# Two partial sums kept apart in a planned attention and MLP kernel: plain stores and a VectorE add for accumulating DMAs, and other landing times in its scheduler

## The chip, the cores and the metric

The kernel runs on one core of a Trainium2 chip. The metric is the device time of one execution in microseconds (us). The engines are named as the profile names them: PE is TensorE (matmuls; PEld are its weight loads), DVE is VectorE, ACT is ScalarE, POOL is GpSimd, and SP is SyncE, which here only issues DMAs.

## The reference

A linear attention block is followed by an MLP with softplus. In sizes: 8 batches, 8 heads, 576 tokens, 64 per head, so 4608 tokens of 512 features; `w_in` is 512 x 2048 and `w_out` 2048 x 512.

```
kv  = einsum('bhsd,bhse->bhde', k, v)
o   = einsum('bhsd,bhde->bhse', q, kv)
x   = o / sqrt(mean(o*o, -1) + 1e-6) * g_norm      # heads joined: 4608 x 512
h   = x @ w_in
g   = max(h, 0) + log1p(exp(-abs(h)))              # softplus
out = g @ w_out                                     # 4608 x 512, float32
```

## The kernel before

**Numbers in three parts.** The large matrices are kept as three parts of type float32r (a high part, the rest, and a correction), made by one ACT operation and two DVE operations, and every large product sums matmuls of such parts in PSUM. The weights come as 64-bit floats. A fetch (L398, 512 KB for a piece of 128 x 512) is followed by a chain on ACT and DVE (L409 to L439) that makes a float32 of them, and by the split.

**Three phases.** The 2048 columns between the two products are cut into 16 chunks of 128.

- The head loads q, k, v and the first weights. For each batch PE sums kv (L671), for each tile of 128 tokens it makes the rows of o (L695), then ACT, DVE and POOL normalise them and PE turns them (L713, L751). This work goes on beside the first phase.
- The first phase (ph 0, function `step`) goes over 12 blocks of 384 tokens, and in each over chunks 0 to 3 (blocks 0 to 3) or 0 to 5 (the others). A step is 12 matmuls for h (L838), softplus and split on ACT and DVE (L849, L853, L860, L862), and 9 matmuls into the sums of three tiles (L845).
- The second and third phases (ph 1 and 2, function `wide_step`; `LAST` is 2) go over 9 blocks of 512 tokens, and in each over pairs of the remaining chunks: 27 steps in the second phase, 21 in the third. A step makes h for two chunks by seven block products (L1025, 42 matmuls) with ACT copies in between (L1049, L1066, L1070) and a DVE add (L1074), then softplus (L1052), the split (L1082, L1085, L1088), and 24 matmuls into the sums of four tiles (L1095). The operands of the seven products are made by `units_of` (loads at L935, split at L985 to L991).

**Partial sums.** A tile's sum (128 x 512 in float32, one PSUM bank) is complete after three phases. `leave` takes a bank to SBUF with ACT (L886). In the first phase SP stores it to a DRAM tile (L906). In the second phase POOL adds it to that DRAM tile with an accumulating DMA (L902). In the third phase `enter` first loads the tile from DRAM (L880, on SP) and ACT copies it into the bank (L881); the matmuls add to it, and `leave` scales and stores the output (L896 or L906). SBUF tiles of 128 x 512 for all of this, for weights and for x come from one ring `m` of 8 slots.

**The planner.** No order is written by hand. Every operation is entered with `add(engine, ns, run, after, pos, take, give, size, ...)`: its engine, its assumed cost, what it depends on, a position `pos`, and the buffer slots that it takes and gives back. `Plan.order` simulates the engines with these costs and, on each engine, starts among the tasks that can start about first the one of lowest `pos`. The instructions are issued in that order, so each engine's queue is fixed when the program is built. For a DMA the planner keeps one clock for all transfers:

```
if t.size:
    dma_free = max(dma_free, at + t.ns) + t.size
    t.end = dma_free + 2000
```

`size` is the time that the transfer is taken to need; `t.end` is when its data count as landed. An SP load into the ring `m` may only start while more than `KEEP` = 4 slots are free. The positions come from lists of tuned numbers, `P0` (weights and head), `P1`, `P2` (later weights) and `P3` (the wide steps). Where the planner finds PE idle for 400 ns in the head, it puts a warm-up matmul (L1176).

Of the kernel before, what the change touches and what calls it, by code (L numbers as in the profile page):

```python
# [8 lines left out]
F32 = mybir.dt.float32  # L9
# [4 lines left out]
ALU = mybir.AluOpType  # L14
# [4 lines left out]
P = 128  # L19
# [36 lines left out]
class Plan:  # L56
# [5 lines left out]
    READY = {"PE": 2500, "ACT": 2500, "DVE": 4000, "POOL": 2500, "SP": 700}  # L62
    SWITCH = {("all", "rows"): 90, ("all", "kv"): 90, ("rows", "all"): 250, ("kv", "all"): 250, ("rows", "kv"): 140, ("kv", "rows"): 140}
    TOGETHER, PATIENCE = 1, 0.0
    KEEP = 4
    BEGIN = 4000
    SOON = 150
# [7 lines left out]
    def slot(self, ring):  # L75
        return Slot(ring)

    def add(self, engine, ns, run, after=(), pos=0.0, take=(), give=(), size=0, behind=None, follows=None, kind="all"):
        t = Task(engine, ns, run, [a for a in after if a is not None], pos, list(take), list(give), size)
        for s in t.give:  # L80
            s.readers += 1
        self.tasks.append(t)
        t.follows = follows
        t.behind = behind
        t.kind = kind
        return t

    def order(self):
# [30 lines left out]
        dma_free = 1500  # L119
# [3 lines left out]
        while left:  # L123
            best = None
            for engine, tasks in ready.items():
                options = []
                for t in tasks:
                    at = max(engine_free[engine], t.ready)
                    if t.size:
                        at = max(at, dma_free - 2500)  # L130
                    for i, s in enumerate(t.take):
                        others = sum(u.ring == s.ring for u in t.take[:i])
                        if engine == "SP" and s.ring in ("m", "n"):
                            others += self.KEEP
                        if len(free[s.ring]) <= others:
                            break
                        at = max(at, sorted(free[s.ring])[sum(u.ring == s.ring for u in t.take[:i])][0])
                    else:
                        options.append((at, t))
                if not options:  # L140
                    continue
                first = min(at for at, _ in options)
                options = [(at, t) for at, t in options if at <= first + self.SOON]
                small = [o for o in options if engine == "PE" and o[1].kind != "all"]
                if small:
                    rest = [o for o in options if o[1].kind == "all"]
                    if kind != "all":
                        options = [o for o in small if o[1].kind == kind] or small
                    elif rest and len(small) < self.TOGETHER and (
                            min(o[1].pos for o in small) + self.PATIENCE > min(o[1].pos for o in rest)):  # L150
                        options = rest
                at, t = min(options, key=lambda o: (o[1].pos, o[0]))
                if engine == "PE" and self.spare and self.spare[-1].start is None:
                    ring, run, ns, _ = self.spare
                    begin = max(engine_free["PE"], self.BEGIN, min(free[ring])[0] if free[ring] else at)
                    if begin + ns <= at:
                        s = Slot(ring)
                        at, t = begin, Task("PE", ns, lambda s=s: run(s), [], None, [s], [s], 0)
                        t.kind = "all"
                        s.readers = 1  # L160
                if best is None or at < best[0]:
                    best = (at, t)
            if best is None:
                raise RuntimeError("the plan is stuck at " + str([(e, t.pos, [s.ring for s in t.take if not free[s.ring]]) for e, ts in ready.items() for t in ts][:20]))
            at, t = best
            if t in ready[t.engine]:
                ready[t.engine].remove(t)
                left -= 1
            for s in t.take:
                place = min(free[s.ring])  # L170
                free[s.ring].remove(place)
                s.place = place[1]
                if t.pos is not None:
                    coming[s.ring] = coming.get(s.ring, 0) - 1
            if t.engine == "PE":
                t.ns += self.SWITCH.get((kind, t.kind), 0)
                kind = t.kind
            t.start = at
            engine_free[t.engine] = at + t.ns
            t.end = at + t.ns + self.HANDOVER[t.engine]  # L180
            if t.size:
                dma_free = max(dma_free, at + t.ns) + t.size
                t.end = dma_free + 2000
            for s in t.give:
                s.readers -= 1
                last_read[id(s)] = max(last_read.get(id(s), 0), t.end)
                if not s.readers:
                    free[s.ring].append((last_read[id(s)], s.place))
                    retire(s.ring)
            for u in users.get(id(t), ()):  # L190
                waiting[id(u)] -= 1
                if not waiting[id(u)]:
                    u.ready = max([a.end for a in u.after] + ([u.follows.start] if u.follows else []), default=0)
                    ready.setdefault(u.engine, []).append(u)
            done.append(t)
# [4 lines left out]
def kernel(  # L200
# [24 lines left out]
    nc = tc.nc  # L225
    B, H, S, D = q.shape
    d_model, d_ff = moe_w_in.shape
# [17 lines left out]
    STEPS = [(ph, n, p) for ph in (1, 2) for n in range(n_wide) for p in PAIRS[ph - 1][n]]  # L245
    LAST = 2

    P0 = [-49.84, -17.88, -35.99, -11.25, -19.79, -5.76, -6.59, 2.32, -72.59, -44.84, -44.11, -27.86, -36.42, -23.37, -11.42, -1.64, 8.39, -28.07, 13.62, 9.21, 8.15, 12.69, -9.98, 5.3, 1.39, 25.83, -11.96, 7.88, 13.2, 7.36]
    CONVERT, FETCH, EARLY, LATER = P0[:8], P0[8:16], P0[16:27], P0[27:]
    P1 = [50.98, 57.72, 60.23, 40.06, 110.11, 134.41, 41.79, 46.64, 73.31, 91.73, 127.74, 138.75]  # L250
    P2 = [23.23, 37.56, 36.87, 47.12, 56.32, 61.0, 53.55, 123.6, 69.05, 107.19, 42.49, 16.95, 48.29, 68.01, 98.48, 79.47, 86.8, 80.78, 146.51, 128.13, -4.65]
    P3 = [2.14, 1.08, 5.88, -0.92, 1.63, 2.67, 2.6, 1.59, 2.29, 2.01, 3.35, 0.34, -0.08, -0.89, 3.05, -0.96]
    SPLIT = {p: (P1[i], P1[6 + i]) for i, p in enumerate((2, 3, 4, 5, 6, 7))}
    TAKEN = {c: (P2[c - 6], P2[4 + c]) for c in range(6, 16)}
    LEAD, APART, AHEAD, MM2, LATE, SPLIT_G = P3[0], P3[1], P3[2], P3[3:11], P3[11:14], P3[14]
# [10 lines left out]
    dram = ctx.enter_context(tc.tile_pool(name="dram", bufs=1, space=DRAM))  # L266
# [39 lines left out]
    slot, add = plan.slot, plan.add  # L306
# [513 lines left out]
    part = {}  # L820
# [54 lines left out]

    def enter(t, bank, pos):

        pt = slot("m")
        src, st = part[t]
        ld = add("SP", 350, lambda: nc.sync.dma_start(out=new(pt, [P, d_model]), in_=src), [st], pos - 2.5, [pt], [], 900, behind=pos - 3.5)  # L880
        return add("ACT", 600, lambda: nc.scalar.copy(new(bank, [P, d_model]), pt.tile), [ld], pos, [bank], [pt])  # L881

    def leave(ph, t, bank, done, pos):

        ot = slot("m")
        a = add("ACT", 690 if ph == LAST else 600, lambda: nc.scalar.activation(  # L886
            new(ot, [P, d_model]), bank.tile, func=AF.Copy, scale=scale if ph == LAST else 1.0),
            [done] + (scale_done if ph == LAST else []), pos, [ot], [bank])
        if ph == LAST and BY_PE <= t < n_tiles - TB:
            n, i = divmod(t, TB)  # L890

            def store():
                for m in range(P // BL):
                    a, u = divmod(P // BL * i + m, TB)
                    row = n * NT + u * P + a * BL
                    nc.sync.dma_start(out=out[row:row + BL], in_=ot.tile[m * BL:(m + 1) * BL])  # L896

            add("SP", 1600, store, [a], pos, [], [ot], 750)
            return
        if ph == 1:  # L900
            dst, st = part[t]
            part[t] = dst, add("POOL", 1000, lambda: nc.gpsimd.dma_start(out=dst, in_=ot.tile, accum_op=ALU.add),  # L902
                               [a, st], pos, [], [ot], 1900)
            return
        dst = out[t * P:(t + 1) * P] if ph == LAST else dram.tile([P, d_model], F32, name=f"part_{t}")
        part[t] = dst, add("SP", 350, lambda: nc.sync.dma_start(out=dst, in_=ot.tile), [a], pos, [], [ot], 720)  # L906

    unit_slots, unit_done = {}, {}

# [234 lines left out]
    for c in range(KF):  # L1144
        for j in (2 * c, 2 * c + 1):
            if c < OWN:
                pos = CONVERT[j] if c < 4 else LATER[c - 4] + LATER[2] * (j % 2)
# [64 lines left out]
```

## Time and profile before

| | us |
|---|---|
| median of 3 runs | 882.69 (879.84 to 883.61) |
| profiled execution | 884.47 |
| its span, first to last instruction | 882.7 |
| first L838 (head ends) | 44.3 |
| first L1025 (second phase begins) | 364 |
| first bank filled again by L881 (third phase begins) | 658.5 |
| last matmul ends | 878.8 |

The phases overlap by a step or so. Rows of the profile give busy time in us, mean ns of one instruction, and idle time of the engine just before, with what ended it. Where the profile gives a stretch of time, it lists for each engine the busy us in it, the granted clock of PE as a share of full speed, and the DMA engines' busy share.

### The profile page before, as it was taken

What the parts mean: (1) busy time and instruction counts of PE and PEld (TensorE: products, weight loads), DVE (VectorE), ACT (ScalarE), POOL (GpSimd) and SP (SyncE); (2) the same over time, 40 slices, a digit from 0 to 9 for tenths busy, and PEclk for the clock granted to TensorE, in tenths of its full rate; (3) what the DMA queues carried; (4) which work ended last, traced back from release to release, by engine and by line L of the source; (5) the groups of instructions that cost most, each with busy time, mean ns of one, the idle gap of its engine ahead of it and who ended that gap; (6) DMA issues with size and microseconds to landing.
All of it is one profiled execution on the core that took longest, in us unless ns stands there. A gap on an engine that the chain in (4) does not pass through costs nothing.

```text
span 882.7 us, 16941 instructions
## 1 busy us (share of the span) xinstructions
PE 861.5 (98%) x6457; PEld 758.8 (86%) x6457; DVE 682.9 (77%) x956; ACT 538.7 (61%) x1015; POOL 111.8 (13%) x115
## 2 busy tenths in 40 slices
PE   7899999999999999999999998999999999999998
PEld 5587888889888899888898887989898888988886
DVE  6798888887878888898889896777887756676652
ACT  5776555444544568666658654556778755666764
POOL 0434223132113100001101100101100000000000
PEclk9999999999999999999999999999999999999999
DMA  9999999859893775537765856846745633566643
GB/s 252 264 199 297 241 221 262 143 179 197 261 165 98 191 215 177 157 105 185 196 186 136 202 153 175 197 128 155 173 132 132 194 96 119 183 193 183 193 120 86
DMA packets 234448, 157.62 MB, mean 179 GB/s; under 512 B 105728, under 2 KB 197888, under 8 KB 234368
## 3 DMA queue, kind: packets, MB, share of 16 engines
q1 hardware_dynamic: 229024, 147.11, 61.3%
q0 software_dynamic: 5184, 9.44, 7.0%
q8 instruction: 50, 0.82, 0.4%
q14 instruction: 30, 0.25, 0.1%
q10 hardware_dynamic: 160, 0.00, 0.0%
HBM read 103.55 MB, written 52.95 MB: 177 GB/s over the span
## 4 chain that ended last, share of the span: by engine, by line
PE 88%; DMA 5%; DVE 3%; ACT 2%; issue 1%; POOL 1%; SPq 0%; DVEq 0%; ACTq 0%
PE banks L1095 30%; PE banks L1025 27%; PE banks L838 14%; PE banks L845 13%; PE banks L695 2%; DMA g<-in_moe_w_out_dram 2%; PE banks L671 2%; DMA raw<-in_moe_w_in_dram 1%; DMA raw<-in_moe_w_out_dram 1%; DMA early<-in_q_dram 1%; PE banks L713 1%; DMA loads<-in_v_dram 1%; POOL r L703 0%; PE banks L751 0%; DVE half L707 0%
## 5 line engine op out<-in xcount | busy, mean ns | idle before, releaser
L1095 PE MATMUL banks<-pieces,gv 128*128 128x512 f32 x624 | 196.0, 395 | 0.0
L1025 PEld LDWEIGHTS banks<-units,pieces 128*128 128x128 f32 x1140 | 151.5, 191 | 16.5 <-ACT banks L1070 6.2
L1025 PE MATMUL banks<-units,pieces 128*128 128x256 f32 x1140 | 158.3, 284 | 4.4 <-ACT banks L1070 3.1
L845 PE MATMUL banks<-pieces,gv 128*128 128x512 f32 x576 | 147.3, 397 | 0.2 <-DVE gv L853 0.2
L838 PE MATMUL banks<-units,pieces 128*128 128x384 f32 x768 | 145.9, 338 | 0.0
L838 PEld LDWEIGHTS banks<-units,pieces 128*128 128x128 f32 x768 | 134.7, 188 | 5.0
L845 PEld LDWEIGHTS banks<-pieces,gv 128*128 128x128 f32 x576 | 105.8, 188 | 21.0 <-DVE gv L853 0.5
L1095 PE MATMUL banks<-pieces,g_False 128*128 128x512 f32 x312 | 122.7, 393 | 0.1
L1095 PEld LDWEIGHTS banks<-pieces,gv 128*128 128x128 f32 x624 | 105.6, 190 | 11.8
L1085 DVE TENSOR_TENSOR gv<-g_True,gv 128x1024 fp32r<-128x1024 f32 x48 | 58.8, 1225 | 67.0 <-ACT gv L1082 66.8
L860 ACT ACTIVATE half<-banks 128x384 f32<-128x384 f32 x64 | 31.3, 489 | 76.4 <-PE banks L838 75.9
L902 POOL DMA_DIRECT2D part<-m x36 | 31.4, 901 | 324.7 <-ACT m L886 289.9
L1095 PEld LDWEIGHTS banks<-pieces,g_False 128*128 128x128 f32 x312 | 58.7, 188 | 13.9 <-ACT banks L1066 0.5
L703 POOL TENSOR_TENSOR r<-r,half 128x8 f32<-128x8 f32 x36 | 64.9, 1804 | 3.0
L1052 ACT ACTIVATE g_True<-banks 128x256 f32<-128x256 f32 x96 | 36.7, 383 | 44.5 <-PE banks L1025 43.0
L1074 DVE TENSOR_TENSOR g_True<-banks,g_True 128x512 f32<-128x512 f32 x48 | 33.1, 689 | 37.9 <-PE banks L1025 24.0
L1088 DVE SCALAR_TENSOR_TENSOR g_False<-gv 128x1024 fp32r<-128x1024 f32 x48 | 58.8, 1225 | 1.6
L985 ACT ACTIVATE units<-loads 128x1024 fp32r<-128x1024 f32 x42 | 44.5, 1059 | 21.3 <-PE banks L1025 17.5
L988 DVE TENSOR_TENSOR units<-loads,units 128x1024 fp32r<-128x1024 f32 x42 | 51.3, 1221 | 5.5 <-ACT units L985 5.3
L991 DVE SCALAR_TENSOR_TENSOR units<-units 128x1024 fp32r<-128x1024 f32 x42 | 51.3, 1222 | 1.4
L1082 ACT ACTIVATE gv<-g_True 128x1024 fp32r<-128x1024 f32 x48 | 50.9, 1060 | 1.0
L886 ACT ACTIVATE m<-banks 128x512 f32<-128x512 f32 x72 | 41.7, 596 | 13.7 <-PE banks L1095 7.5
(117 smaller groups left out, 1370.3 us busy)
## 6 DMA issues: line engine op xcount, KB each, us to landing
loads<-x SPq DMA_DIRECT2D x180, 128.0 KB, 2.7
loads<-form SPq DMA_DIRECT2D x45, 256.0 KB, 3.1
part<-m SPq DMA_DIRECT2D x36, 256.0 KB, 3.3
form<-loads SPq DMA_DIRECT2D x36, 256.0 KB, 3.0
part<-m POOLq DMA_DIRECT2D x36, 256.0 KB, 5.2
m<-part SPq DMA_DIRECT2D x36, 256.0 KB, 3.0
raw<-in_moe_w_in_dram SPq DMA_DIRECT2D x16, 512.0 KB, 5.5
loads<-in_k_dram SPq DMA_DIRECT2D x32, 256.0 KB, 4.8
```

Of the source, the lines that this page charges most:

```text
L703: nc.gpsimd.tensor_tensor(out=r.tile, in0=r.tile, in1=half, op=ALU.pow)
L838: nc.tensor.matmul(hp, lhsT=w_in.tile[:, i, kd * P:(kd + 1) * P], rhs=xv.tile[:, i, kd], start=(m == 0), stop=(m == 3 * KD - 1))
L845: nc.tensor.matmul(mine[i].tile, lhsT=gv.tile[:, m, i * P:(i + 1) * P], rhs=w_out.tile[:, m], start=(c == cs[0] and m == 0), stop=(c == cs ...
L886: a = add("ACT", 690 if ph == LAST else 600, lambda: nc.scalar.activation(new(ot, [P, d_model]), bank.tile, func=AF.Copy, scale=scale if p ...
L985: nc.scalar.activation(part_of(0, F32R), xl.tile if m > 1 else xl.tile[:, 0], func=AF.Copy, scale=DOWN)
L988: nc.vector.tensor_tensor(out=part_of(1, F32R), in0=xl.tile if m > 1 else xl.tile[:, 0], in1=part_of(0), op=ALU.subtract)
L991: nc.vector.scalar_tensor_tensor(out=part_of(2, F32R), in0=part_of(1), scalar=-RADIX, in1=part_of(0), op0=ALU.mult, op1=ALU.add)
L1025: nc.tensor.matmul(place(q), lhsT=w[:, m, at:at + P], rhs=dst.tile[:, m, v, kd] if u < 6 else dst.tile[:, m, kd], start=(u == 0 and not m ...
L1082: nc.scalar.activation(gvt(0, F32R), gt(), func=AF.Copy, scale=DOWN)
L1085: nc.vector.tensor_tensor(out=gvt(1, F32R), in0=gt(), in1=gvt(0), op=ALU.subtract)
L1088: nc.vector.scalar_tensor_tensor(out=gt(F32R), in0=gvt(1), scalar=-RADIX, in1=gvt(0), op0=ALU.mult, op1=ALU.add)
L1095: nc.tensor.matmul(mine[i].tile, lhsT=(gvt(m, F32R) if m < 2 else gt(F32R))[:, c, i * P:(i + 1) * P], rhs=outs[c].tile[:, m], start=fresh ...
```

## The change

Four things are changed.

1. `leave` in the second phase no longer uses POOL: SP stores the sum to a DRAM tile of its own (`part1_t` beside `part0_t`).
2. `enter` in the third phase loads both tiles into two slots of the ring `m`, and DVE adds them into the bank; the ACT copy is gone.
3. The planner counts a DMA as landed 3500 ns after its transfer, not 2000, once its DMA clock is past 60 us.
4. All tuned positions have other values, so the order on every engine differs from the start.

```diff
+    LANDING, FILLED = 3500, 60000
...
-                t.end = dma_free + 2000
+                t.end = dma_free + (self.LANDING if dma_free > self.FILLED else 2000)
...
-    P0 = [-49.84, -17.88, -35.99, ...
+    P0 = [-48.16, -11.59, -36.23, ...
...
-    P1 = [50.98, 57.72, 60.23, ...
+    P1 = [49.25, 55.64, 61.04, ...
...
     def enter(t, bank, pos):
 
-        pt = slot("m")
-        src, st = part[t]
-        ld = add("SP", 350, lambda: nc.sync.dma_start(out=new(pt, [P, d_model]), in_=src), [st], pos - 2.5, [pt], [], 900, behind=pos - 3.5)
-        return add("ACT", 600, lambda: nc.scalar.copy(new(bank, [P, d_model]), pt.tile), [ld], pos, [bank], [pt])
+        both_of = []
+        for src, st in part[t]:
+            pt = slot("m")
+            both_of.append((pt, add("SP", 350, lambda pt=pt, src=src: nc.sync.dma_start(out=new(pt, [P, d_model]), in_=src),
+                                    [st], pos - 2.5, [pt], [], 900, behind=pos - 3.5)))
+        (p0, l0), (p1, l1) = both_of
+        return add("DVE", 700, lambda: nc.vector.tensor_tensor(out=new(bank, [P, d_model]), in0=p0.tile, in1=p1.tile, op=ALU.add),
+                   [l0, l1], pos, [bank], [p0, p1])
 
     def leave(ph, t, bank, done, pos):
...
-        if ph == 1:
-            dst, st = part[t]
-            part[t] = dst, add("POOL", 1000, lambda: nc.gpsimd.dma_start(out=dst, in_=ot.tile, accum_op=ALU.add),
-                               [a, st], pos, [], [ot], 1900)
-            return
-        dst = out[t * P:(t + 1) * P] if ph == LAST else dram.tile([P, d_model], F32, name=f"part_{t}")
-        part[t] = dst, add("SP", 350, lambda: nc.sync.dma_start(out=dst, in_=ot.tile), [a], pos, [], [ot], 720)
+        dst = out[t * P:(t + 1) * P] if ph == LAST else dram.tile([P, d_model], F32, name=f"part{ph}_{t}")
+        st = add("SP", 350, lambda: nc.sync.dma_start(out=dst, in_=ot.tile), [a], pos, [], [ot], 720)
+        part.setdefault(t, []).append((dst, st))
```

The lines of the changed kernel stand one lower than before from there on: L1095 becomes L1096, L1025 becomes L1026, the loads of `enter` are at L882 and its add at L885.

More of the change, by code (lines that the diff above doesn't have):

```diff
@@ L246 @@
     LAST = 2
-    P0 = [-49.84, -17.88, -35.99, -11.25, -19.79, -5.76, -6.59, 2.32, -72.59, -44.84, -44.11, -27.86, -36.42, -23.37, -11.42, -1.64, 8.39, -28.07, 13.62, 9.21, 8.15, 12.69, -9.98, 5.3, 1.39, 25.83, -11.96, 7.88, 13.2, 7.36]
+    P0 = [-48.16, -11.59, -36.23, -9.34, -21.88, -6.03, 0.48, 3.73, -72.34, -30.1, -41.26, -15.18, -39.67, -26.8, -3.81, 5.27, 8.4, -26.81, 14.38, 10.02, 8.24, 12.88, -11.53, 5.44, 1.19, 33.13, -14.12, 6.15, 11.68, 7.45]
     CONVERT, FETCH, EARLY, LATER = P0[:8], P0[8:16], P0[16:27], P0[27:]
-    P1 = [50.98, 57.72, 60.23, 40.06, 110.11, 134.41, 41.79, 46.64, 73.31, 91.73, 127.74, 138.75]
-    P2 = [23.23, 37.56, 36.87, 47.12, 56.32, 61.0, 53.55, 123.6, 69.05, 107.19, 42.49, 16.95, 48.29, 68.01, 98.48, 79.47, 86.8, 80.78, 146.51, 128.13, -4.65]
-    P3 = [2.14, 1.08, 5.88, -0.92, 1.63, 2.67, 2.6, 1.59, 2.29, 2.01, 3.35, 0.34, -0.08, -0.89, 3.05, -0.96]
+    P1 = [49.25, 55.64, 61.04, 40.09, 109.45, 133.28, 49.73, 28.85, 72.45, 98.22, 131.85, 140.31]
+    P2 = [24.13, 36.89, 36.77, 47.57, 55.58, 67.77, 58.81, 116.43, 78.93, 120.62, 44.24, 19.49, 49.95, 77.41, 122.0, 83.32, 80.75, 86.17, 164.23, 141.39, -6.45]
+    P3 = [1.62, 1.24, 5.47, 0.83, 2.68, 2.58, 4.22, 2.0, 2.57, 2.99, 3.06, 1.5, 1.16, 0.45, 2.4, -0.72]
     SPLIT = {p: (P1[i], P1[6 + i]) for i, p in enumerate((2, 3, 4, 5, 6, 7))}
```

## The prediction

> **What bounds the kernel now.** I read the page's busy times first, then busy time by stretch, then the waits and the timeline of TensorE (PE). The page:
>
> ```profile
> PE 861.5 (98%) x6457; PEld 758.8 (86%) x6457; DVE 682.9 (77%) x956; ACT 538.7 (61%) x1015; POOL 111.8 (13%) x115
> ```
>
> PE is the bound engine, so a change is worth only the PE time that it fills or spares. The matmuls stay the same, so I look for PE's empty time by stretch (head, first phase, second phase in three pieces, third phase, tail). Columns: length, then busy us of PE, weight loads, VectorE (DVE), ScalarE (ACT), GpSimd (POOL), then the granted clock, the DMA engines' share, GB/s:
>
> ```profile
> 0.00:44.30 44.30, 33.89 (x359) 24.34 (x360) 31.96 (x57) 27.31 (x51) 10.15 (x15) 0.92 0.99 258
> 44.30:364.30 320.00, 317.67 (x2940) 279.83 (x2939) 269.93 (x459) 177.98 (x351) 70.25 (x64) 1.00 0.82 201
> 364.30:530.00 165.70, 164.44 (x1035) 147.18 (x1034) 144.66 (x183) 108.53 (x205) 15.80 (x18) 1.00 0.63 167
> 530.00:545.00 15.00, 11.85 (x65) 10.31 (x64) 7.41 (x11) 6.62 (x13) 1.73 (x2) 0.89 0.79 188
> 545.00:652.00 107.00, 107.00 (x669) 95.70 (x668) 84.30 (x103) 65.48 (x124) 10.38 (x12) 1.00 0.61 154
> 652.00:878.80 226.80, 226.65 (x1400) 201.48 (x1399) 144.67 (x147) 152.04 (x273) 3.45 (x4) 1.00 0.52 150
> ```
>
> The third phase is full (0.15 us empty): whatever ACT is spared there buys nothing. The second phase is full but for 1.26 us before 530 and the stretch 530 to 545, where 3.15 us stand empty and the clock falls to 0.89. Pricing each matmul at its line's median interval between starts (0.119 us for L1025, 0.232 for L1095), 520 to 540 runs 4.9 us over: 3.3 empty, the rest slow matmuls. 360 to 380 runs 1.5 over, 680 to 700 0.6; everything else in phases two and three is within 0.1. So about **7 us** can be had there. All matmuls but the warm-up's sum to 833.4 us at these prices, 49.3 below the span: 29.2 in the head (44.3 long, 15.1 of work that counts), 3.9 after the last matmul, these 7, and so some 9 in the first phase, nearly all in small matmuls and changes between them; its waits for other engines are 2.3 us. The 4.9 us, in the timeline (the bracket is idle time and what ended it):
>
> ```profile
> 525.71 0.86 POOL L902 DMA_DIRECT2D part<-m  x1 [22.82 <-ACT m L886]
> 525.72 0.38 SPq L398 DMA_DIRECT2D raw<-in_moe_w_out_dram  x1
> ...
> 533.26 0.66 ACT L409 ACTIVATE sq<-raw 128x512 bf16<-128x512 bf16 x1 [4.53 <-DMA raw<-in_moe_w_out_dram]
> ...
> 533.83 0.36 ACT L1070 COPY banks<-banks 128x256 f32<-128x256 f32 x1
> ...
> 534.24 1.31 PE L1025 MATMUL banks<-units,pieces 128*128 128x256 f32 x6 [3.15 <-ACT banks L1070]
> ```
>
> A weight fetch was issued together with an accumulating store from POOL, took 7.5 us, and its reader L409 stood on ACT ahead of L1070, for which PE waits. The planner had counted 450 + 1800 + 2000 ns for it, 4.25 us. What such transfers take (KB each, us from issue to landing):
>
> ```profile
> part<-m SPq DMA_DIRECT2D x36, 256.0 KB, 3.3
> part<-m POOLq DMA_DIRECT2D x36, 256.0 KB, 5.2
> m<-part SPq DMA_DIRECT2D x36, 256.0 KB, 3.0
> raw<-in_moe_w_out_dram SPq DMA_DIRECT2D x8, 512.0 KB, 5.2
> ```
>
> [...] six L1025 matmuls took 1.31 us after the gap, 0.88 us usually. [...] L1074, with 512 columns and an operand in PSUM, shows 689.
>
> **The change part by part.**
> 1. Second phase: 36 accumulating DMAs leave POOL (0.86 us each there, 31 us, on an idle engine: nothing gained). Their queue has 7.0% of 882.7 us over 36, 1.7 us of all 16 DMA engines each. In their place SP issues 36 plain stores: 0.38 us each on SP (median of L906), 14 us over 287. Each uses about 0.96 us of the DMA engines (61.3% of 882.7 us for 147.1 MB, times 0.262 MB): 27 us less DMA time, so the share falls from 63% to about 54%. SP is in order, so loads and fetches now queue behind a store that waits for ACT L886 (26 such waits before, 33 us in all); the planner can place them, and the loads are fetched ahead. The m slot is free after 3.3 us instead of 5.2. Worth nothing by itself on PE but shorter landings.
> 2. Third phase: 36 ACT copies (0.591 us, 21 us) become 36 DVE adds. DVE goes from 144.7 busy us of 226.8 to 169.5 (75%), ACT from 152 to 131. The add's row is not in the trace (two SBUF operands, PSUM written): 0.69 by L1074, at least the 0.59 of the copy, at most the 1.22 of a 1024-column add, which would be 44 us and 83% of DVE; I take 0.69. Following each bank through the trace, the copy ended 5.7 us (median) before the bank's first matmul, in four of 36 cases under 2.1 us, least 0.9. An add can stand behind one 1.22 us operation; the cover holds but for those four. I charge 0.5 us.
> 3. Third phase: 36 more loads on SP (0.42 us each, 15 us over 227) and 35 us of DMA time (52% to about 67%). The ring m has 8 slots and SP must leave 4 (KEEP), so of the eight tiles that a block of four sums needs, four are there early and the rest are loaded when adds give slots back. The built program's SP queue shows it: loads in groups of two to four between the output stores. Chain for the last two sums: add 0.7, issue 0.4 to 0.8, landing 3.0, add 0.7, about 5 us. In the trace the first two copies of a block come about 5 us before the last two and 9 before the last bank's first matmul. It fits, with some 4 us to spare.
> 4. LANDING: after 60 us the planner counts 3.5 us instead of 2. In program order, the PE work between the fetch and its reader on ACT, for the ten weight fetches of phase two, priced by the matmul rows: before 9.2, 5.6, 5.9, 5.2, 4.2, 7.1, 3.4 (the one that stalled), 7.5, 4.1, 10.3 us; after 8.8, 4.7, 8.1, 9.5, 10.6, 5.5, 6.2, 7.5, 5.9, 6.4. With a landing near 5.2 none should hold PE: **-4.9**. The 1.4 at 372 (five ACT operations ahead of L1066) and the 0.5 at 688 stand in an order that is written anew: **-1.9**. Late next would be the 4.7 one, about 1 us.
> 5. First phase: the same PE work and 80 changes of kind for 81. The one DMA wait there (1.2 us, a v load) should go: **-1**, from -3 to +3 for the new order.
> 6. Head: the new positions give 17.3 us of PE work ahead of the first L838 (15.1 before), but DVE has 36.9 us of work up to the third L621, which gates it, instead of 33.7. With the same DVE idle time it comes 3.2 later with 2.2 more done: **+1**, from -5 (DVE idles 10.3 us there) to +3. Six more warm-up matmuls (0.21 us each) are inside that.
>
> Sum: -4.9 - 1.9 + 0.5 - 1 + 1 = **-6.3 us**. The profiled execution took 884.47 us (span 882.7 and 1.8 around it), so 878.2; the median of the runs, 882.69, is 1.8 below it, so **876.4 us**.
>
> **The rivals.**
> *Another wait takes the place of the one removed.* ACT and DVE are in order, every engine's order is new, and one late landing cost 4.9. For it: fetches took up to 8.0 us and the smallest distance is 4.7. Against: of ten such fetches before, one stalled PE. Then -1 to -2: 881.
> *The head or first phase gains.* DVE waits for weight fetches early; if half of its 10.3 us is filled: 5 to 6 less, 870.5.
> *The third phase stalls (slower).* In DVE's new queue the add often stands right before L1085, which gates the next step's second matmuls. The late pair's loads have 2 to 5 us of PE work between issue and add, a landing has 3.0 to 4.7. If DVE stands 1.3 us past PE's cover at each of the eight handovers between blocks, 10.4 us are lost: 887 or more. The point is the 4 us to spare of step 3: landings near 7 us (as POOL's worst of 7.7 before), or loads held up on SP. For it: PE has no slack of its own there. Against: PE's work there hid every copy.
> *The change doesn't do what it says:* landing times are only the planner's; if positions rule the order, the stall may stay. This counts with the first rival.
>
> **How the numbers follow.** My forecast 0.60, its own range 872 to 880.5; new wait 0.18; head gains 0.07; slower 0.15. 0.5% is 4.4 us, about what a measurement of this kernel can tell from no change: faster is below 878.3. Eight tenths of the forecast lie there (0.48) and the head's gain: 0.55. Same: 0.12 and 0.18, 0.30. Slower 0.15. Range: 869 for the head's gain to 887, where the stalls of the third phase begin to count.
>
> **What would show it.** Right: no drop of the clock and no PE gap over 1 us after 364, POOL's rows L902 gone, ACT's waits for raw short, DVE near 75% and PE full in the third phase; first L838 near 47 us. Wrong: gaps before L1096 or L1026 in the third phase ended by DVE, adds that wait for m<-part, or a first phase longer than 320 us.

## The result, and the profile after

| | before | after |
|---|---|---|
| median of 22 runs each, us | 882.7 | 880.69 |
| lowest and highest | 879.84 to 885.2 | 878.9 to 884.29 |
| profiled execution, its span | 884.47, 882.7 | 881.73, 878.6 |
| first L838 (after: L839) | 44.3 | 47.7 |
| last matmul ends | 878.8 | 874.7 |

The ratio after to before is 0.9979, 95% interval 0.9969 to 0.9989: about 2 us faster, not 6.3. The two profiled spans differ by 4.1 us, twice as much as the medians; the two profiled executions differ by 2.7, since that of after took 3.1 us outside its span and that of before 1.8. How much of the 4.1 is usual for these kernels is the key to the case.

In the page of after, PE is still the bound engine; DVE has 36 instructions more, ACT and POOL have 36 fewer each:

```profile
PE 858.5 (98%) x6463; PEld 757.6 (86%) x6463; DVE 704.3 (80%) x992; ACT 519.5 (59%) x979; POOL 80.1 (9%) x79
```

The stretches of after, with the same columns as in the prediction (length, busy us of PE, weight loads, DVE, ACT and POOL, clock, DMA share, GB/s), the head and the first phase cut at 47.7 and 360:

```profile
0.00:47.70 47.70, 34.31 (x428) 24.48 (x428) 35.89 (x64) 29.24 (x57) 10.16 (x15) 0.96 0.96 244
47.70:360.00 312.30, 310.50 (x2853) 273.78 (x2846) 260.48 (x444) 172.45 (x338) 69.90 (x64) 1.00 0.81 200
360.00:530.00 170.00, 169.59 (x1064) 152.21 (x1064) 147.97 (x189) 111.77 (x212) 0.00 (x0) 1.00 0.54 172
530.00:545.00 15.00, 15.00 (x97) 13.60 (x96) 10.43 (x11) 7.25 (x14) 0.00 (x0) 1.00 0.41 132
545.00:650.00 105.00, 105.00 (x656) 94.11 (x655) 85.96 (x107) 66.06 (x127) 0.00 (x0) 1.00 0.54 171
650.00:874.70 224.70, 224.05 (x1381) 199.43 (x1379) 163.55 (x181) 132.08 (x234) 0.00 (x0) 1.00 0.62 191
```

The second phase is full: only 0.41 us stand empty from 360 to 650, and the stretch 530 to 545 is 15.00 of 15.00 at full clock. POOL is idle there, and the DMA share fell from 0.63 to 0.54 as worked out. The third phase has 0.65 us empty, where before had 0.15. DVE is at 163.55 of 224.7, 73% (forecast 75%), ACT at 132 (forecast 131), the DMA share at 0.62 (forecast about 0.67). The transfers, in the page's list of DMA issues (count, KB each, us to landing):

```profile
part<-m SPq DMA_DIRECT2D x72, 256.0 KB, 3.0
m<-part SPq DMA_DIRECT2D x72, 256.0 KB, 3.3
raw<-in_moe_w_in_dram SPq DMA_DIRECT2D x16, 512.0 KB, 5.2
```

The pairs of loads land in 3.3 us (median; 5.6 at worst), where step 3 counted on 3.0 and the slower rival on 3.0 to 4.7. The add itself is at L885, in the list of groups (busy, mean ns | idle before):

```profile
L885 DVE TENSOR_TENSOR banks<-m,m 128x512 f32<-128x512 f32 x36 | 24.8, 695 | 8.2 <-ACT m L891 6.3 <-DMA m<-part 0.9 <-ACT banks L1067 0.8
```

It takes 695 ns, against the 0.69 us that the prediction took from L1074, an add of the same size with one operand in PSUM (689 ns in before; as L1075, 690 in after). It waited for a load once, 0.9 us; its other waits are for ACT, nearly all for emptying the bank (L891).

### The profile page after: what moved, and what is told of

The parts are those of the page before. It is cut to its first block, busy times and chain, and to the rows that moved or that the text cites. A ratio compares the mean times of both kernels' runs of the same rounds, so it can differ in the third digit from the quotient of the medians.

```text
span 878.6 us, 16974 instructions
## 1 busy us (share of the span) xinstructions
PE 858.5 (98%) x6463; PEld 757.6 (86%) x6463; DVE 704.3 (80%) x992; ACT 519.5 (59%) x979; POOL 80.1 (9%) x79
## 4 chain that ended last, share of the span: by engine, by line
PE 91%; DMA 2%; DVE 2%; ACT 2%; SPq 1%; issue 1%; POOL 0%; DVEq 0%; ACTq 0%
PE banks L1096 30%; PE banks L1026 26%; PE banks L846 15%; PE banks L839 15%; PE banks L696 2%; PE banks L672 2%; DMA raw<-in_moe_w_in_dram 1%; SPq L742 1%; DMA early<-in_q_dram 1%; PE banks L714 1%; DMA loads<-in_v_dram 1%; DVE half L708 0%; ACT w L778 0%; POOL r L704 0%; SPq L661 0%
## 5 line engine op out<-in xcount | busy, mean ns | idle before, releaser
L1096 PE MATMUL banks<-pieces,gv 128*128 128x512 f32 x552 | 173.0, 394 | 0.0
L1026 PEld LDWEIGHTS banks<-units,pieces 128*128 128x128 f32 x1212 | 159.1, 190 | 11.0 <-ACT banks L1071 2.0
L1026 PE MATMUL banks<-units,pieces 128*128 128x256 f32 x1212 | 166.2, 282 | 0.7 <-ACT banks L1067 0.4
L846 PE MATMUL banks<-pieces,gv 128*128 128x512 f32 x576 | 146.4, 397 | 0.0
L839 PE MATMUL banks<-units,pieces 128*128 128x384 f32 x768 | 145.6, 338 | 0.1
L839 PEld LDWEIGHTS banks<-units,pieces 128*128 128x128 f32 x768 | 135.0, 188 | 5.1 <-ACT pieces L505 0.2
L846 PEld LDWEIGHTS banks<-pieces,gv 128*128 128x128 f32 x576 | 105.8, 188 | 20.9
L1096 PE MATMUL banks<-pieces,g_False 128*128 128x512 f32 x276 | 108.3, 392 | 0.4 <-DVE g_False L1089 0.4
L1096 PEld LDWEIGHTS banks<-pieces,gv 128*128 128x128 f32 x552 | 95.1, 189 | 13.4 <-DVE banks L885 0.4
L1086 DVE TENSOR_TENSOR gv<-g_True,gv 128x1024 fp32r<-128x1024 f32 x48 | 58.7, 1223 | 40.9 <-ACT gv L1083 40.7
L1096 PE MATMUL banks<-w,gv 128*128 128x512 f32 x216 | 67.7, 394 | 0.0
L1096 PEld LDWEIGHTS banks<-pieces,g_False 128*128 128x128 f32 x276 | 51.8, 188 | 12.5 <-ACT banks L1071 0.8
L989 DVE TENSOR_TENSOR units<-loads,units 128x1024 fp32r<-128x1024 f32 x42 | 51.2, 1220 | 11.4 <-ACT units L986 11.2
L1089 DVE SCALAR_TENSOR_TENSOR g_False<-gv 128x1024 fp32r<-128x1024 f32 x48 | 58.7, 1224 | 1.4
L1075 DVE TENSOR_TENSOR g_True<-banks,g_True 128x512 f32<-128x512 f32 x48 | 33.1, 690 | 24.8 <-PE banks L1026 18.9
L850 DVE TENSOR_TENSOR gv<-half,gv 128x384 fp32r<-128x384 f32 x64 | 35.1, 549 | 20.3 <-ACT gv L863 19.4
L891 ACT ACTIVATE m<-banks 128x512 f32<-128x512 f32 x72 | 42.2, 596 | 15.4 <-PE banks L1096 9.5
```

Of the source, the lines that this page charges most:

```text
L839: nc.tensor.matmul(hp, lhsT=w_in.tile[:, i, kd * P:(kd + 1) * P], rhs=xv.tile[:, i, kd], start=(m == 0), stop=(m == 3 * KD - 1))
L846: nc.tensor.matmul(mine[i].tile, lhsT=gv.tile[:, m, i * P:(i + 1) * P], rhs=w_out.tile[:, m], start=(c == cs[0] and m == 0), stop=(c == cs ...
L989: nc.vector.tensor_tensor(out=part_of(1, F32R), in0=xl.tile if m > 1 else xl.tile[:, 0], in1=part_of(0), op=ALU.subtract)
L1026: nc.tensor.matmul(place(q), lhsT=w[:, m, at:at + P], rhs=dst.tile[:, m, v, kd] if u < 6 else dst.tile[:, m, kd], start=(u == 0 and not m ...
L1086: nc.vector.tensor_tensor(out=gvt(1, F32R), in0=gt(), in1=gvt(0), op=ALU.subtract)
L1089: nc.vector.scalar_tensor_tensor(out=gt(F32R), in0=gvt(1), scalar=-RADIX, in1=gvt(0), op0=ALU.mult, op1=ALU.add)
```

## The experiments

PE has 833.4 us of useful matmuls at the prediction's prices in every one of these kernels. The time that PE lost up to a given matmul is that matmul's start less the work before it. Cut at the first L838, the first L1025 (at 347.4 in the first profile of before; at the 364 given earlier the second phase has taken over for the most part) and the first matmul of wide step 27, it gives the table below (us, from one profile each; "third" runs to the last matmul). L1025 and L1066 of before are L1026 and L1067 in after; in a kernel with extra lines ahead of them they stand higher, by three in reader_later and three_moves and by 19 in sums_same_order. A row is one execution and need not be a usual one: the profile of three_moves was the second fastest of its 22 runs, that of sums_only the third slowest of 22.

| kernel | head | first phase | head and first | second | third |
|---|---|---|---|---|---|
| before, the profile of the prediction | 29.2 | 9.2 | 38.4 | 6.5 | 0.5 |
| before_again | 31.1 | 9.9 | 41.0 | 2.2 | 0.5 |
| before_third | 29.9 | 11.4 | 41.3 | 1.7 | 0.6 |
| after | 30.5 | 8.9 | 39.4 | 0.4 | 1.6 |
| after_again | 29.9 | 9.2 | 39.1 | 0.5 | 1.7 |
| after_beside | 30.2 | 8.7 | 38.9 | 0.5 | 1.7 |
| sums_only | 31.6 | 11.3 | 42.9 | 1.7 | 1.3 |
| order_only | 28.6 | 10.4 | 39.0 | 2.0 | 0.6 |
| landing_only | 28.4 | 14.8 | 43.2 | 7.2 | 5.4 |
| reader_later | 31.2 | 9.3 | 40.5 | 1.5 | 0.6 |
| sums_same_order | 31.8 | 9.9 | 41.7 | 2.1 | 7.4 |
| three_moves | 29.6 | 9.0 | 38.6 | 1.4 | 0.6 |

**The same kernels again.** before_again, before_third and after_again are unchanged kernels, profiled once more.

> The kernel before, profiled a second time. Theory one (the first profile caught a worse case than the usual run): the stall of PE near 530 us costs less than the 4.9 us seen there, 0 to 3 us, and the span is near 881. Theory two (the stall is in the order and so in every run): about 4.9 us lost there again, span within 1 us of 882.7.

> The kernel before, profiled a third time. If the first profile was a worse case: 0 to 2 us lost near 530; first L838 anywhere from 43.5 to 46.7. If a stall of some us is usual: 3 us or more.

> The changed kernel, profiled a second time. If its order has no short fetch left: second phase within 1 us of full again, third phase 1 to 2 us short of full, the head 45.5 to 48. If its first profile was merely a lucky one: a gap of over 1 us in the second phase.

They took 882.8, 882.75 and 880.25 us. The fetch that cost 4.9 us in the first profile is in the timeline of before_again:

```profile
528.00 0.35 SPq L398 DMA_DIRECT2D raw<-in_moe_w_out_dram  x1
528.21 0.86 POOL L902 DMA_DIRECT2D part<-m  x1 [22.81 <-ACT m L886]
...
533.08 0.67 ACT L409 ACTIVATE sq<-raw 128x512 bf16<-128x512 bf16 x1 [1.85 <-DMA raw<-in_moe_w_out_dram]
533.66 0.37 ACT L1070 COPY banks<-banks 128x256 f32<-128x256 f32 x1
534.09 0.97 PE L1025 MATMUL banks<-units,pieces 128*128 128x256 f32 x6 [0.49 <-ACT banks L1070]
```

The instructions and the order on each engine are the same, but the fetch landed after 5.1 us instead of 7.5. PE stood 0.49 us instead of 3.15, and the six matmuls took 0.97, not 1.31. In before_third it was 4.6 us:

```profile
533.01 0.67 ACT L409 ACTIVATE sq<-raw 128x512 bf16<-128x512 bf16 x1 [1.42 <-DMA raw<-in_moe_w_out_dram]
```

The stretch 520 to 540 lost 0.7 and 0.3 us in these two. **The 4.9 us were one execution's, not the usual price of the order.** One thing beside the fetch differs: in the slow execution POOL's store was issued 0.01 us ahead of it, in the other two 0.21 us behind it. Whether that made it slow was not tried. The gap at 372, which stands in an order and not in a landing, is another matter: 1.4 us are lost there in all three profiles of before.

**Each part alone.** sums_only has the code of `enter` and `leave` from after, with before's positions and 2000 ns (points 1 and 2 of the change, by their hunks of its diff); order_only has after's positions and 3500 ns, with before's `enter` and `leave` (points 3 and 4, by the others); landing_only changes the landing time and nothing else:

```diff
+    LANDING, FILLED = 3500, 60000
...
-                t.end = dma_free + 2000
+                t.end = dma_free + (self.LANDING if dma_free > self.FILLED else 2000)
```

> The changed storing of the partial sums alone (plain stores on SP, two loads, the add on DVE), with the positions and the 2000 ns of before. Theory one (POOL's accumulating transfers delay the weight fetches): no PE gap over 1 us in the second phase, 5 us less there, 878 to 880. Theory two (the planner's order did it, storing is neutral or costs): gaps of several us stay somewhere in the second phase or come in the third, 882 to 886.

> The positions and the landing time of the changed kernel, with POOL's accumulating stores and the ACT copy of before. Theory one (POOL's transfers delay the fetches): a PE gap over 1 us beside them in the second phase, 882 to 885. Theory two (the order did it): second phase full, some 6 us less than before there, 879 to 881; the head costs 1 to 4 us more than before in both.

> The kernel before with landings counted 3500 ns after the transfer once past 60 us, positions unchanged. If the landing time alone clears the stall: second phase 5 us shorter, head as before (its first 60 us are planned alike), 877 to 880. If the positions are what matters: the order is merely another one, with other gaps, 881 to 887.

Measured: sums_only 882.9 us, ratio 0.9984 (0.9971 to 0.9997); order_only 881.74, 0.9979 (0.9963 to 0.9994); landing_only 895.81, 1.0125 (1.0104 to 1.0146), against 883.92 of before beside them. The halves gain 1.0 and 2.2 us, against 2.0 of the whole change in the result and 3.5 in after_beside, which ran on the same chip as these three; the intervals are too wide to rank them or to say whether they add.

The table says more than the times, though each row is one execution. In the second phase neither half does it alone: sums_only keeps the gap at 372 (1.4 us) and order_only has a new one (1.0 us at 442, below), while the three profiles of after lose 0.4 to 0.5. So the expectation that the order alone would fill this phase was wrong. In the third phase the kernels with adds lose more: 1.3 in sums_only and 1.6 to 1.7 in after, against 0.5 to 0.6 with ACT copies (before and order_only). The adds themselves have little of it, as the next section shows. The head and first phase go with the positions: 39.0 in order_only and 38.9 to 39.4 in after, 42.9 in sums_only.

landing_only is 12 us slower, more than either side of its expectation allowed, and loses in all three phases (14.8, 7.2 and 5.4 in the table). The later landing is thus not a gain in itself. The new positions ran only with 3500 (after and order_only), so what they would do with 2000 stays open.

What POOL's stores can cost is seen in order_only, in its timeline: a split on DVE waited for a ring slot that an accumulating store still read. PE waits for DVE five us later; whether the one led to the other was not tried.

```profile
436.85 0.69 DVE L487 TENSOR_TENSOR m<-m,pieces 128x512 f32<-128x512 f32 x1 [1.63 <-DMA part<-m]
...
442.11 0.50 PE L1096 MATMUL banks<-pieces,g_False 128*128 128x512 f32 x1 [0.76 <-DVE g_False L1089]
```

**The late fetch's reader moved.** reader_later is before with L409 of that fetch two ACT operations later, behind L1070 and L886. The orders of PE, DVE and SP are the same.

```diff
+    tasks = plan.order()
+    a1, d3 = squares[31][1:]
+    i = tasks.index(a1)
+    behind = [n for n, t in enumerate(tasks) if n > i and t.engine == "ACT"][1]
+    tasks.insert(behind + 1, a1)
+    tasks.pop(i)
+    for t in tasks:
```

> The kernel before with one instruction moved: on ACT, the reader L409 of the weight fetch that stalled PE near 530 stands two ACT operations later, behind L1070, for which PE waits. All else is in the same order. If the stall is in every run as the first profile showed it: 4.9 us less, a ratio of 0.9945. If the usual landing is near 5 us, as in the second profile (0.7 us lost there): 0.5 to 2 us less, a ratio of 0.998 to 0.9995.

881.94 us against 883.28, ratio 0.9988 (0.9972 to 1.0004). In its timeline the copy that PE waits for now runs ahead of the reader, and nothing is lost there:

```profile
532.53 0.36 ACT L1073 COPY banks<-banks 128x256 f32<-128x256 f32 x1 [1.70 <-PE banks L1028]
...
533.72 0.66 ACT L410 ACTIVATE sq<-raw 128x512 bf16<-128x512 bf16 x1
```

The stall that the prediction priced at 4.9 us is worth some 1 us in the median (1.3 here), and the interval reaches past zero.

**The sums without a new order.** sums_same_order keeps before's order on every engine, task by task; each accumulating store becomes a plain store from SP at the same place, each ACT copy a DVE add, with the second tile loaded right after the add two places earlier.

```diff
+        def first_load():
+            nc.sync.dma_start(out=new(pt, [P, d_model]), in_=src)
+            if t < 2:
+                second_load(t)
+        def both():
+            nc.vector.tensor_tensor(out=new(bank, [P, d_model]), in0=pt.tile, in1=second(t), op=ALU.add)
+            if t + 2 < n_tiles:
+                second_load(t + 2)
...
-        return add("ACT", 600, lambda: nc.scalar.copy(new(bank, [P, d_model]), pt.tile), [ld], pos, [bank], [pt])
+        return add("ACT", 600, both, [ld], pos, [bank], [pt])
...
-            part[t] = dst, add("POOL", 1000, lambda: nc.gpsimd.dma_start(out=dst, in_=ot.tile, accum_op=ALU.add),
+            part[t] = dst, add("POOL", 1000, lambda: nc.sync.dma_start(out=part1[t], in_=ot.tile),
```

> The kernel before with every engine's order kept, and only the operations on the partial sums exchanged: where POOL issued the accumulating store, SP issues a plain one; where ACT copied, DVE adds two tiles. The second tile of each pair lies in the buffer of the weight fetches, which is free by then, and is loaded right after the add two places earlier. If POOL's transfers slowed the fetch: PE loses less than 1.5 us at 530, and with a third phase that costs nothing 1 to 4 us less. If the add costs: PE gaps in the third phase ended by DVE, 1 to 10 us, total 882 to 890.

888.4 us, ratio 1.0073 (1.0047 to 1.0098). Its second phase lost 2.1 us, like the second phases of before_again and before_third, and its fetch at 528.76 landed for the reader at 533.76, 5.0 us. With POOL's store 0.2 us behind it the fetch took 5.1 and 4.6, so a POOL transfer beside the fetch is not enough to make it slow, and storing apart shows no gain there. This is one execution without POOL; what made the one fetch take 7.5 stays open. The third phase lost 7.4 us. In its timeline an add waits for its second tile, PE waits for a DVE result behind it, and ACT waits for loads that stand late in SP's queue:

```profile
700.75 0.70 DVE L894 TENSOR_TENSOR banks<-m,seconds 128x512 f32<-128x512 f32 x1 [2.25 <-DMA seconds<-part]
702.10 0.97 PE L1044 MATMUL banks<-turned,half 128*128 128x256 f32 x6 [0.88 <-DVE g_True L1093]
...
793.61 1.06 ACT L1004 ACTIVATE early<-loads 128x1024 fp32r<-128x1024 f32 x1 [3.46 <-DMA loads<-form]
794.98 0.96 PE L1044 MATMUL banks<-units,pieces 128*128 128x256 f32 x6 [1.02 <-ACT g_True L1068]
```

This is the prediction's slower rival at work, so its mechanism is real. after escapes it, and so does sums_only (1.3 us lost), whose orders were planned with the adds and the loads in them. But sums_same_order also has only two buffers for the second tiles, and loads one only when an earlier add is done; order and buffers were not told apart.

**Three instructions moved.** three_moves is reader_later with, besides, the two splits L476 that ran on ACT ahead of L1066 at 372 put behind it and behind L1049. after_beside is the changed kernel on the same chip.

```diff
+    highs = [t for t in tasks if t.engine == "ACT" and t.run.__name__ == "high" and abs(t.pos - 73.46) < 0.06]
+    copy = next(t for t in tasks if t.engine == "ACT" and t.run.__name__ == "v_copy" and abs(t.pos - 66.62) < 0.005)
+    for t in highs:
+        tasks.remove(t)
+    i = tasks.index(copy)
+    tasks[i + 1:i + 1] = highs
```

> The kernel before with three ACT instructions in other places and nothing else: the reader L409 of the late fetch as in reader_later, and the two splits L476 that stood ahead of the copy L1066 at 372 us put behind it and behind L1049; their readers on DVE come late enough in either order. Theory (the second phase of before has about 1.4 us in the fixed order at 372 and on average about 1 us, not 4.9, in the late fetch): the gap before L1025 at 372 falls from 1.26 to about 0.4 us, the second phase loses about 0.5 to 1 us instead of 1.5 to 2.2 in the plain executions, and the time is about 2 us below before, ratio 0.9975 to 0.9985: the same as the whole change, without a sum stored apart. Rival (the change's gain lies in the first phase and the head, whose order it makes anew, not in the second): the gap at 372 falls likewise but the ratio stays near that of reader_later, 0.9988 or nearer to 1, and the changed kernel beside it on the same chip is faster by 1 us or more.

> The changed kernel itself, on the same chip and against the same runs of the kernel before as three_moves. Theory: ratio 0.997 to 0.999, within 1 us of three_moves. Rival: faster than three_moves by 1 us or more.

three_moves: 882.47 us, ratio 0.9982 (0.9967 to 0.9997). after_beside: 880.77, ratio 0.9961 (0.9944 to 0.9977), against 884.3 of before. The gap at 372 itself fell as expected, in the timeline of before and then of three_moves:

```profile
372.20 0.98 PE L1025 MATMUL banks<-units,pieces 128*128 128x256 f32 x6 [1.26 <-ACT banks L1066]
```

```profile
371.62 0.98 PE L1028 MATMUL banks<-units,pieces 128*128 128x256 f32 x6 [0.45 <-ACT banks L1069]
```

But the second phase as a whole did not gain by it. It lost 1.4 us, where 0.5 to 1 was expected and reader_later had lost 1.5: the ACT operations behind the two moved splits now come later, and PE loses the time again in pieces of 0.1 to 0.2 us up to 377. So the price of the order at 372 is not shown by this run.

after is 1.7 us faster than three_moves, which the rival expectation had asked for. The two intervals against before overlap a little, but 13 of the 22 runs of three_moves took longer than the longest of after_beside's 17. So moving three instructions gives about half of the gain (1.8 of 3.5 us, with wide intervals). Of the rest, the table has 1 us in the second phase (1.4 to 0.4 or 0.5), but the third phase takes it back (0.6 to 1.7). What is left should lie in the head and first phase; the profile of three_moves, a fast one, does not show it (38.6), so it is read from all the executions. Matched matmul by matmul, the seven executions with before's positions and 2000 ns reach the end of the first phase up to 4.5 us apart; the three of after, and order_only with the same order on PE there, stay within 0.5. One place where they part is near 140 us, a wait for a load of v. In the timeline of the first profile of before, then of before_third, then of after:

```profile
138.98 0.69 PE L671 MATMUL banks<-loads 128*64 128x64 f32 x16 [1.21 <-DMA loads<-in_v_dram]
139.60 2.34 PE L845 MATMUL banks<-pieces,gv 128*128 128x512 f32 x9
```

```profile
140.82 0.69 PE L671 MATMUL banks<-loads 128*64 128x64 f32 x16 [1.72 <-DMA loads<-in_v_dram]
141.43 3.75 PE L845 MATMUL banks<-pieces,gv 128*128 128x512 f32 x9
```

```profile
142.28 1.16 PE L696 MATMUL banks<-early,w 64*64 64x64 f32 x64
143.37 1.15 PE L672 MATMUL banks<-loads 128*64 128x64 f32 x32
144.45 3.75 PE L839 MATMUL banks<-units,pieces 128*128 128x384 f32 x20
```

PE waits for v loads in the first phase in all seven executions of before's positions, 1.2 to 3.0 us in sum. In before_third and sums_only the clock fell around the wait near 140 too (0.89 in 135 to 150): in before_third nine L845 matmuls then took 3.75 us, not 2.34. In after the rows of o (L696) stand ahead of these loads' matmuls, and the three executions waited 0, 0.3 and 0 us for v in the whole phase. That is not all gain: the first phase without its v waits lost 8.0 and 8.1 us in the first two profiles of before, and 8.7 to 9.0 in after. In order_only, whose head came 1.8 us earlier with the same order, PE waited 1.4 us for that load and kept almost nothing of its lead. Moving this load alone was not tried, so its share of the gain is read from traces, not shown by an edit.

## Why the prediction was wrong in size

The forecast said -6.3 us. The spans of the two first profiles show -4.1, the medians -2.0; different errors lie in these two steps.

- **Step 4, the term of -4.9: the step that failed.** The mechanism was there, but the term was sized by one execution, and what is usual is about 1 us. On the first pair of profiles it came out as written: the second phase fell from 6.5 to 0.4 us lost, -6.1 for the -6.3 of its two terms there (4.9 and 1.4). But that place costs 0.7 and 0.3 us in the other two profiles of before, and reader_later, which takes it away, gains some 1 us. That one execution's 884.47 stood 1.8 us above the median. The prediction took that 1.8 from both kernels; but it was a surplus of waits in that execution of before alone (its row of the table sums to 45.4 us, those of before_again and before_third to 43.7 and 43.6). The time outside the span is not a fixed 1.8 either: it was 3.1 in the first profile of after.
- **Step 4, the term of -1.9: half of it came.** At 372 the loss fell from 1.4 to 0.57, a gain of 0.8. In place of the 0.5 at 688 the new order has two stalls at 676 and 685 that cost 1.1 us (below), so there it lost.
- **Steps 1 and 3, the queues and loads: right.** The second phase's DMA share and POOL's rows are as worked out, and an add waited for m<-part only once, 0.9 us. after's ACT shows no wait for raw at all after 338.
- **Step 2, the adds: cheaper than charged.** Forecast +0.5. The third phase did go from 0.5 lost to 1.6 or 1.7 in all three profiles of after, but only 0.2 of it, at 867.5, ends on an add. The larger part is in these two places of after's timeline, the same in all three profiles:

```profile
674.91 1.06 ACT L986 ACTIVATE early<-loads 128x1024 fp32r<-128x1024 f32 x1
675.87 0.36 ACT L1050 COPY g_True<-banks 128x256 f32<-128x256 f32 x1
676.29 2.41 PE L1026 MATMUL banks<-units,pieces 128*128 128x256 f32 x18 [0.26 <-ACT g_True L1050]
...
682.08 0.68 DVE L493 SCALAR_TENSOR_TENSOR m<-m,pieces 128x512 f32<-128x512 f32 x1
682.68 1.22 DVE L1086 TENSOR_TENSOR gv<-g_True,gv 128x1024 fp32r<-128x1024 f32 x1
683.93 1.22 DVE L1089 SCALAR_TENSOR_TENSOR g_False<-gv 128x1024 fp32r<-128x1024 f32 x1
685.30 0.47 PE L1096 MATMUL banks<-pieces,g_False 128*128 128x512 f32 x1 [0.39 <-DVE g_False L1089]
```

DVE runs no add between 661.7 and 688.5. At 676 an operand split on ACT (L986) stands ahead of the copy that PE waits for, at 685 a weight split on DVE (L493) ahead of the pair L1086 and L1089. So the prediction's sign of being wrong, gaps ended by DVE, did come, but no add stood there. order_only, planned with ACT copies at the same positions, has neither stall; moving these operations in after was not tried.

- **Step 5, the first phase: right direction, too small.** The v load's wait did go, though its share of the gain is not shown by an edit. On the first pair the phase gained only 0.3, since that profile had drawn the smallest v wait of the seven. Against before_again and before_third the head and first phase together gained about 2 (41.0 and 41.3 to 38.9 to 39.4).
- **Step 6, the head: no net change.** The first L838 came at 47.7, as forecast (near 47), with 17.3 us of work done. But the same order of before puts it at 43.5 to 46.9 in different executions, so the +1 is inside its own noise; over three profiles each, the head lost 30.1 and 30.2.

A sum from ordinary executions, before_again and before_third against the three of after: head and first phase 41.15 to 39.1, second 1.95 to 0.5, third 0.55 to 1.7. That is -2.0 - 1.5 + 1.1 = -2.4 us, and the two measured differences are -2.0 and -3.5. Against these two, the first profile of before stood 4.5 us too long in its second phase and 2.7 us too little in its head and first phase, and the prediction took both for the kernel.

Of the rivals, "another wait takes the place" named 881, near the measured number, but that was luck: its reason did not occur, since no fetch held ACT in after's second phase. The slower rival did not occur in after, though sums_same_order shows that it can.

## What to carry to other kernels

Here the stall that stands in a fixed order came back in every profile (1.4 us, three times), and the stall that hangs on a landing did not (4.9, 0.7 and 0.3). So profile such a stall two or three times before it is priced, and read a profiled run above the median as a sign that a bad one may have been caught. When one execution is the only one at hand, list every wait on a DMA that could have been longer or shorter, in the phases that look good too. Taking a gap away can move it: three_moves filled 0.8 us at 372 and lost nearly all of it again within 5 us. And in a planned kernel the parts belong together: the landing time alone, or the operations alone in the old order, turned a gain of 0.2% into a loss of 1.3 and 0.7%.

## What the runs showed of the hardware

- The same 512 KB fetch, in the same place of the same order, took 4.6 (before_third), 5.1 (before_again) and 7.5 us (the first profile of before) to land.
- The planner's fixed 2000 ns stand behind a transfer. In the first profile of before, the packets of 14 weight fetches can be told from all others: the first one started 1.0 to 2.7 us after the issue (median 1.5), and the landing followed the end of the last one by 0.3 to 1.5 us (median 0.5). So more time went ahead of the data than behind them; what made it so was not shown.
- The first L838 started between 43.5 us (landing_only) and 46.9 us (sums_same_order) with the same order of instructions on PE: the 28.4 and 31.8 us lost in the head, by the table, and 15.1 us of work.
- A wait of 1.7 to 1.8 us between small matmuls was sometimes followed by a fall of PE's clock and sometimes not. In 135 to 150 before_again stood 1.84 us at one go and its granted clock was 1.00; before_third stood 1.72 and its granted clock was 0.89. In the first profile of before the granted clock was 0.50 from 534.7 to 538.1, after a gap of 3.15 us. So the longer of the two waits near 140 kept the clock and the shorter one did not; what decides it was not shown. The two stretches, before_again first (the clock is the third number from the end):

```profile
135.00:150.00 15.00, 13.16 (x151) 11.59 (x151) 13.35 (x24) 8.85 (x17) 3.02 (x2) 1.00 0.87 226
```

```profile
135.00:150.00 15.00, 13.28 (x143) 11.32 (x143) 12.91 (x22) 8.26 (x16) 3.01 (x2) 0.89 0.92 243
```
